# Attention units two at a time: transposes, evictions and values reordered in the first stage of a fused attention and MLP kernel

## The chip, the cores and the metric

The kernel runs on one core of a Trainium2 chip. Its time is the device time of one execution, in microseconds (us). The engines are TensorE (PE in the profile; its weight loads are listed apart as PEld), VectorE (DVE), ScalarE (ACT), GpSimd (POOL) and SyncE (SP, which issues the DMAs). Each engine takes its instructions in the order of its own queue and waits on semaphores for the others. [...]

## What is computed

An attention block with a bias that depends on position, then an MLP with a squared ReLU. Cut to what matters:

```python
B, H, S, D = 4, 8, 576, 64            # hidden size of the bias net 32
scores = q @ k.T / sqrt(D)
x = log1p(abs(i - j)) / log1p(max(i, 1))
bias = relu(x[..., None] @ w1 + b1) @ w2      # one value per head, i, j
attn = softmax(scores + bias)
x = (attn @ v) reordered to (B * S, H * D)
out = relu(x @ w_in) ** 2 @ w_out             # (2304, 512), d_ff 2048
```

## The kernel before

The attention is cut into 80 **units** (b, hp, ic): a batch, a pair of heads and a chunk of 128 query rows. The fifth chunk (`TAIL`) has only 64 rows and holds both heads in one tile. The first 40 units (`NA`) belong to batches 0 and 1 and run chunk by chunk: units 0 to 7 are tail chunks, units 8 to 15 chunk 0, and so on to unit 39. The other 40 units belong to batches 2 and 3 and run in a second stage, in which the preparation of the MLP's weights is mixed in. The MLP follows.

One unit goes through these steps. `score_products` (L404) puts the scores of two heads into four PSUM banks (tile `sp`, one buffer) with eight instructions of 64 rows each, both row halves of TensorE at once. `softmax` (L426) then does two things per head: a VectorE instruction (L431) adds the bias, keeps the result in `t` (two buffers) and finds the maximum, and a ScalarE instruction (L436) takes the exponential into `p` and sums it up. Two units later `transposes` (L494) turns `p` with nine 128 by 128 transposes on TensorE into three banks (`pp` twice with four each, `pa` with one), and ScalarE copies each to `pt` (L802). One unit later `values` (L511) multiplies `pt` by `v` into a bank `px` with twenty instructions of 64 columns each, both column halves of TensorE at once, and VectorE copies the result out (L530, ScalarE for units 0 to 7). After the last chunk of a head pair the sums are inverted, split into three bf16 parts by GpSimd, turned into rows by TensorE (L461), spread by TensorE (L483) and multiplied in by VectorE (L489).

The **bias** is made beside this, for 72 blocks (ic, jb) of 128 rows by 32 columns, `todo` in the code. `bias_mask` (L359) compares distances with thresholds on VectorE and leaves a 0/1 mask (three buffers). `bias_sum` (L374) multiplies the mask by weights on TensorE (16 instructions into a bank `bb`), ScalarE evicts one half with a scale (L386), VectorE multiplies the other half by position factors `xc` (L387), and GpSimd adds both into the bias table (L395). `bias_upto` (L560) makes the mask of the next block ahead of the sum of each block. Units of one chunk need all 18 blocks of that chunk.

In the stage of the first 40 units, the loop at L788, the order on each engine is left to the scheduler of the framework, which moves instructions past each other where data allow it. PSUM has eight banks: four hold `sp`, four are one rotating set for `bb`, `pp`, `pa`, `px` and the rest. The second stage (L966) stands under `tc.manual_schedule()`: there each engine takes the instructions in the order of the program, and the four banks have fixed names a, b, c and d. Jobs of the second stage are placed by `fill` (L833), which holds a budget of time per engine and step.

Of the kernel before, what the change touches and what calls it, by code (L numbers as in the profile page):

```python
# [77 lines left out]
def attention_then_relu2_mlp(ctx: ExitStack, tc: tile.TileContext, q, k, v, cols, w_in, w_out, psi, xmat, dist, out):  # L78
# [13 lines left out]
    def bank(name, tag=None):  # L92
        if tag is None:
            return bank_p["p"].tile([128, 512], F32, name=name, tag="aux", bufs=4)
        return bank_p["p"].tile([128, 512], F32, name=name, tag=tag, bufs=1)
# [275 lines left out]
        DVE.tensor_tensor(out=out, in0=win, in1=th, op=ALU.is_ge)  # L371
        mask_t[ic, jb] = m

    def bias_sum(ic, jb):  # L374
        m = mask_t.pop((ic, jb))
        bb = bank("bb")
        t = prep.tile([128, H, 32], F32, name="bt1", tag="bt1", bufs=BB)
        s = prep.tile([128, H, 32], F32, name="bt2", tag="bt2", bufs=BB)
        for r in range(8):
            for n in range(2):  # L380
                PE.matmul(bb[:, 64 * (7 - r):64 * (8 - r)], lhsT=m[:, r], rhs=wmov[:, n], start=(n == 0), stop=(n == 1))  # L381
        xv = xc_t[ic][:, 32 * jb:32 * jb + 32].rearrange("p (g j) -> p g j", j=4).unsqueeze(1)
# [4 lines left out]
        DVE.tensor_tensor(out=tv, in0=bv[:, 0], in1=xv.to_broadcast([128, H, 8, 4]), op=ALU.mult)  # L387
        if ic == TAIL:
# [6 lines left out]
        POOL.tensor_tensor(out=dst, in0=tw, in1=sw, op=ALU.add)  # L395

    def tail_bias(x, e, lo, hi, copy):
        src = tail_sum[64 * x:64 * x + 64, HP * e:HP * e + HP, lo:hi]
# [24 lines left out]
                tc.keep_in_program_order(mm)  # L423
        return negm, sps

    def softmax(u, n, negm, sp):  # L426
        b, hp, ic = units[u]
        p, sums = p_t[u], sum_t[b, hp]
        bias = bias_t[:, 9 * hp + 2 * ic + n]
        t = att.tile([128, S], F32, name="t", tag="t", bufs=TB)  # L430
        DVE.tensor_tensor_reduce(  # L431
            out=t.rearrange("p (x n) -> p x n", x=2), in0=sp[:, :, :HALF],
            in1=bias.rearrange("p (x n) -> p x n", x=2), scale=-0.125, scalar=3.0e38,
            op0=ALU.add, op1=ALU.min, accum_out=negm[:, n:n + 1],
        )
        ACT.activation(out=p[:, S * n:S * n + S], in_=t, func=AF.Exp, bias=negm[:, n:n + 1], scale=-1.0, accum_out=sums[:, 2 * ic + n:2 * ic + n + 1])  # L436
        if ic == TAIL:
            POOL.tensor_copy(out=p[:, S:S + 64], in_=p[:, S - 64:S])

    begun = {}  # L440

# [49 lines left out]
    def scale_x(b, hp, rows_t):  # L491
        times_rows(b, hp, *spread_rows(rows_t))

    def transposes(u, tags=(None, None, None)):  # L494
        n = 2 if units[u][2] < TAIL else 1
        p = p_t.pop(u)
        pt = att.tile([128, 9, 128], F32, name="pt", tag="pt", bufs=2)
        copies = []
        for h in range(n):
            pp = bank("pp", tags[h])  # L500
            for c in range(4):
                k0 = h * (S + 64) + 128 * c
                PE.transpose(pp[:, 128 * c:128 * c + 128], p[:, k0:k0 + 128], ident)  # L503
            copies.append((pt[:, 4 * h:4 * h + 4], pp.rearrange("p (c m) -> p c m", c=4)))
        pa = bank("pa", tags[2])
        PE.transpose(pa[:, :128], p[:, S - 64:S + 64], ident)  # L506
        copies.append((pt[:, 8], pa[:, :128]))
        pt_t[u] = pt
        return copies

    def values(u, tag=None):  # L511
        b, hp, ic = units[u]
        pt, vt = pt_t.pop(u), v_t[b, hp]
        w = 64 if ic == TAIL else 128
        px = bank("px", tag)
        for c in range(5):
            for h in range(2):
                if c == 4:
                    src = pt[:, 8, 64 * h:64 * h + 64] if ic == TAIL else pt[:, 8, :w]
                else:  # L520
                    src = pt[:, c, 64 * h:64 * h + 64] if ic == TAIL else pt[:, 4 * h + c, :w]
                PE.matmul(px[64 * h:64 * h + 64, :w], lhsT=vt[:, c, h], rhs=src, start=(c == 0), stop=(c == 4))  # L522
        end = S if ic == TAIL else 128 * ic + 128
        return xT[b][:, hp, end - w:end], px[:, :w]

    def keep_values(u, dst, src):
        if u < XC:
# [30 lines left out]
    done = 0  # L558

    def bias_upto(n):  # L560
        nonlocal done
        while done < min(n, len(todo)):
            if done + 1 < len(todo):
                bias_mask(*todo[done + 1])
            bias_sum(*todo[done])
            done += 1

    with tc.manual_schedule():
        late, main = theta_steps(512, S), theta_steps(0, 512)[:2] + theta_steps(0, 128)[2:]
# [215 lines left out]
        return ic == (chunks[-1] if u < NA else NIC - 1)  # L785

    rest = theta_steps(128, 512)[2:]
    for s in range(NA):  # L788
        loads(s)
        scores(s)  # L790
        if s and rest:
            tc.keep_in_program_order(rest.pop(0)())
        if s < AB * HP * TAIL:
            n, r = divmod(s, AB * HP)
            if r == 7 and n + 2 < NIC:
                tc.keep_in_program_order(scale_xc(chunks[n + 2]))
            bias_upto(NJB * n + BO[r])
            if r == 1 and n + 2 < NIC:
                load_xc(chunks[n + 2])
        if s >= TL:  # L800
            for dst, src in transposes(s - TL):
                ACT.copy(dst, src)  # L802
        u = s - TL - 1
        if u >= 0:
            keep_values(u, *values(u))
            b, hp, ic = units[u]
            if ends(u):
                waiting.append((b, hp, normalise(b, hp)))
            if waiting and waiting[0][:2] != (b, hp):
                scale_x(*waiting.pop(0))  # L810

    prep_stack.close()
    half_stack.close()
    aux_stack.close()
    bank_stack = ExitStack()
    bank_p["p"] = bank_stack.enter_context(tc.tile_pool(name="bank", bufs=1, space=PSUM, reuse_waits="tile"))
    pre = ctx.enter_context(tc.tile_pool(name="pre", bufs=1, side="left", reuse_waits="tile"))
# [4 lines left out]
    jobs, norms = [], []  # L822
    room = {}

    def lag(a, b):
# [23 lines left out]

    def norm_job(u):  # L850
        b, hp, ic = units[u]
        st = {"s": sum_t.pop((b, hp))}
        job(
            u + 1,
            ("DVE", 0.4, lambda: norm_inverse(st["s"])),
            ("POOL", 1.3, lambda: st.update(parts=norm_parts(st["s"])), u + TL + (u < NA)),
            ("ROW", 0.24, lambda: st.update(rows=norm_copy(norm_rows(st["parts"], "c"))), u + TL + 2 + (u < NA)),
            ("PE", 0, lambda: st.update(r=spread_rows(st["rows"], ("a", "b"))), u + TL + 2 + (u < NA)),
            ("LAST", 0.9, lambda: times_rows(b, hp, *st["r"])),
        )  # L860
        jobs.insert(len(norms), jobs.pop())
        norms.append(jobs[len(norms)])
# [27 lines left out]
    def scaled(ps_col):  # L890
        wscale.extend(power_of(ps_col))
        for n in range(AB):
            job(now[0] + 1, ("DVE", 0.16, lambda n=n: power_job(now[0] + 1, overall(xcols[n]), lambda c: x_scaled(n, c))))

    xcols = [column(HP) for _ in range(AB)]

    def x_job(at, n):
        job(at, *(("DVE", 0.67, lambda c=c: x_largest(n, xcols[n], (c,))) for c in range(HP)))

    def x_scaled(n, ps_col):  # L900
        scale_of(n, ps_col)
# [64 lines left out]
    with tc.manual_schedule():  # L966
        job(NA + 1, *(("DVE", 0.68, lambda k=k: scan(k)) for k in range(NF)))
        x_job(NA + 4, 0)
        x_job(NA + 7, 1)
        for u in range(NA - TL - 1, NA):  # L970
            norm_job(u)
        for s in range(NA, NU + TL + 2):
            now[0] = s
            full = s < NU and units[s][2] < TAIL
# [6 lines left out]
            if s < NU:  # L981
                negm, sps = score_products(s, False)
            fill(s, 3)
            copies = transposes(s - TL, ("a", "b", "c")) if s - TL < NU else []
            for n in range(2):
                for c in copies[n:n + 1 if n == 0 else None]:
                    ACT.copy(*c)  # L987
                if n:
                    px = values(s - TL - 1, "d") if s - TL - 1 < NU else None
# [8 lines left out]
            fill(s, 1)  # L998
            fill(s, 2)
            if px:  # L1000
                keep_values(s - TL - 1, *px)
    assert not jobs
    kq_stack.close()
    att_stack.close()
# [266 lines left out]
```

## Time and profile before

| | us |
|---|---|
| median of three runs | 731.0 (730.5 to 731.05) |
| the profiled execution | 731.07 |
| its span, first to last instruction | 729.0 |
| TensorE busy in the span | 701.5 |
| VectorE busy | 554.2 |
| ScalarE busy | 474.9 |
| GpSimd busy | 183.0 |
| granted clock of TensorE, mean | 0.992 |

How to read it: a row of the timeline begins with its start in us from the span's beginning, then its length in us, the engine, the line of the kernel, the operation, output and inputs, the shape, and how many instructions are merged. In square brackets stands how long the engine had been idle just before, and what released it. "Issue" is time in which the engine waited for nothing that the profile shows. Matmuls are pipelined, so each of them lasts longer than the distance to the next start. Distances between starts are what they cost in a row.

### The profile page before, as it was taken

Reading aid. Unit: us, or ns where it says so; the run is one execution under the profiler, and the core shown is the slowest. Engines: PE = TensorE matmul, PEld = TensorE weight load, DVE = VectorE, ACT = ScalarE, POOL = GpSimd, SP = SyncE. Lnnn points to the kernel's source line nnn. Section 1 sums busy time; section 2 is a strip of 40 time slices with the busy share of each in tenths; the row PEclk is TensorE's granted clock in tenths of the full one; section 3 lists DMA queues with packets and bytes.
Section 4 is the critical chain, followed back from the end, with each engine's and each line's share of the span. In section 5 each row is a group of like instructions: output and inputs, shape, how many; then the busy total and the mean of one; then the engine's idle time right before and its main releaser. Section 6 shows DMA issues by size and latency. Waiting matters only on the chain.

```text
span 729.0 us, 17376 instructions
## 1 busy us (share of the span) xinstructions
PE 701.5 (96%) x6966; PEld 565.1 (78%) x6966; DVE 554.2 (76%) x1181; ACT 474.9 (65%) x954; POOL 183.0 (25%) x297
## 2 busy tenths in 40 slices
PE   7799999999999999999999999999999999999992
PEld 6577777777777776777878888888888888888881
DVE  8998888865588789898898969868568775567661
ACT  5678777777677788888667657676465664454220
POOL 6563333331110146343421403212021112000000
PEclk9999999999999999999999999999999999999996
DMA  6630000004467421400623324050057313533100
GB/s 186 204 115 3 18 2 3 2 2 120 164 235 251 105 86 52 131 31 30 215 90 160 144 115 160 1 218 1 1 187 284 117 49 113 205 116 116 58 2 29
DMA packets 31620, 75.13 MB, mean 103 GB/s; under 512 B 5556, under 2 KB 13876, under 8 KB 30516
## 3 DMA queue, kind: packets, MB, share of 16 engines
q1 hardware_dynamic: 31540, 74.03, 29.7%
q8 instruction: 55, 0.90, 0.5%
q14 instruction: 25, 0.20, 0.1%
HBM read 55.66 MB, written 18.35 MB: 102 GB/s over the span
## 4 chain that ended last, share of the span: by engine, by line
PE 85%; DVE 8%; ACT 3%; issue 2%; DMA 0%; ACTq 0%; DVEq 0%
PE y L1147 26%; PE ha L1052 12%; PE px L522 11%; PE sp L421 11%; PE hb L1052 9%; PE pp L503 9%; PE bb L381 4%; DVE mask L371 2%; PE pa L506 2%; ACT p L436 1%; DVE t L431 1%; DVE bt L387 1%; ACT pt L987 1%; PE ra L483 1%; DVE wa L198 0%
## 5 line engine op out<-in xcount | busy, mean ns | idle before, releaser
L1052 PEld LDWEIGHTS <-area 128*128 128x128 f16 x1680 | 147.7, 98 | 24.8 <-issue 8.8
L1147 PE MATMUL y<-w,gh 128*128 128x512 f32 x576 | 149.2, 398 | 1.1 <-ACT gh L1091 1.1
L431 DVE CUSTOM_DVE_ANT_0 t<-sp,area 128x576 f32<-128x576 f32 x144 | 103.7, 754 | 27.7 <-PE sp L421 24.2
L1147 PEld LDWEIGHTS y<-w,gh 128*128 128x128 f32 x576 | 105.1, 188 | 23.3 <-ACT gh L1091 2.1
L436 ACT ACTIVATE p<-t,negm 128x576 f32<-128x576 f32 x144 | 111.9, 779 | 11.0 <-DVE negm L431 10.7
L421 PE MATMUL sp<-k,q 64*128 64x288 f32 (+1 forms) x640 | 98.6, 425 | 0.9 <-DVE negm L431 0.4
L522 PE MATMUL px<-pt,v 128*64 128x128 f32 (+1 forms) x1600 | 96.8, 267 | 1.5 <-DVE bt L387 0.7
L522 PEld LDWEIGHTS px<-pt,v 128*64 128x64 f32 x1600 | 79.2, 137 | 16.5 <-issue 6.9
L1052 PE MATMUL ha<-area 128*128 128x256 f16 (+1 forms) x816 | 85.4, 260 | 0.0
L503 PE MATMUL pp<-ident,p 128*128 128x128 f32 x576 | 82.4, 280 | 1.3 <-DVE bt L387 1.0
L1147 PE MATMUL y<-w,gl 128*128 128x512 f32 x288 | 79.0, 390 | 0.0
L503 PEld LDWEIGHTS pp<-ident,p 128*128 128x128 f32 x576 | 61.5, 141 | 19.7 <-issue 7.2
L395 POOL TENSOR_TENSOR area<-bt,bt 128x256 f32<-128x256 f32 x72 | 53.6, 767 | 78.5 <-DVE bt L387 78.5
L421 PEld LDWEIGHTS sp<-k,q 64*128 64x128 f32 (+1 forms) x640 | 52.6, 175 | 20.4 <-issue 6.8
L1052 PE MATMUL hb<-area 128*128 128x256 f16 (+1 forms) x612 | 64.9, 260 | 0.0
L1147 PEld LDWEIGHTS y<-w,gl 128*128 128x128 f32 x288 | 54.1, 188 | 12.2 <-DVE gl L1092 0.2
L987 ACT COPY pt<-pp 128x512 f32<-128x512 f32 x76 | 44.0, 579 | 27.7 <-PE pp L503 27.4
L371 DVE TENSOR_TENSOR mask<-sdist,theta 128x1024 f16<-128x1024 f16 x81 | 55.9, 727 | 5.6 <-PE bb L381 5.3
L381 PEld LDWEIGHTS <-mask 128*128 128x128 f16 x1296 | 42.3, 100 | 12.2 <-DVE mask L371 6.7
L381 PE MATMUL bb<-wmov,mask 128*128 128x64 f16 x1296 | 47.5, 196 | 4.3 <-DVE mask L371 4.1
L802 ACT COPY pt<-pp 128x512 f32<-128x512 f32 x68 | 37.7, 587 | 14.5 <-PE pp L503 14.5
L1092 DVE TENSOR_TENSOR gl<-area,gh 128x512 fp32r<-128x512 f32 (+1 forms) x40 | 25.3, 668 | 26.0 <-ACT gh L1091 24.2
(163 smaller groups left out, 987.8 us busy)
## 6 DMA issues: line engine op xcount, KB each, us to landing
raw<-in_w_in SPq DMA_DIRECT2D x32, 512.0 KB, 4.3
r<-in_w_out SPq DMA_DIRECT2D x16, 512.0 KB, 5.1
xs<-area SPq DMA_DIRECT2D x4, 1792.0 KB, 13.3
py<-o SPq DMA_DIRECT2D x12, 512.0 KB, 3.5
o<-py SPq DMA_DIRECT2D x12, 512.0 KB, 4.3
v<-in_v SPq DMA_DIRECT2D x16, 320.0 KB, 4.1
q<-in_q SPq DMA_DIRECT2D x32, 128.0 KB, 2.8
out<-o SPq DMA_DIRECT2D x8, 512.0 KB, 2.9
```

Source lines behind the costliest of these rows:

```text
L371: DVE.tensor_tensor(out=out, in0=win, in1=th, op=ALU.is_ge)
L381: PE.matmul(bb[:, 64 * (7 - r):64 * (8 - r)], lhsT=m[:, r], rhs=wmov[:, n], start=(n == 0), stop=(n == 1))
L395: POOL.tensor_tensor(out=dst, in0=tw, in1=sw, op=ALU.add)
L421: mm = PE.matmul(out_t[to, x, :HALF], lhsT=qt[rows, cols], rhs=kt[rows, k0:k0 + HALF], start=True, stop=True)
L431: DVE.tensor_tensor_reduce(out=t.rearrange("p (x n) -> p x n", x=2), in0=sp[:, :, :HALF], in1=bias.rearrange("p (x n) -> p x n", x=2), sca ...
L436: ACT.activation(out=p[:, S * n:S * n + S], in_=t, func=AF.Exp, bias=negm[:, n:n + 1], scale=-1.0, accum_out=sums[:, 2 * ic + n:2 * ic + n ...
L503: PE.transpose(pp[:, 128 * c:128 * c + 128], p[:, k0:k0 + 128], ident)
L522: PE.matmul(px[64 * h:64 * h + 64, :w], lhsT=vt[:, c, h], rhs=src, start=(c == 0), stop=(c == 4))
L802: ACT.copy(dst, src)
L987: ACT.copy(*c)
L1052: PE.matmul(h[:, s, :w], lhsT=a, rhs=x, start=(k == 0), stop=(k == 5))
L1147: PE.matmul(y_t[n][k], lhsT=(gl if m == 2 else gh)[:, slot, o:o + 128], rhs=wl if m == 1 else wh, start=((n, P) in firsts and f == 0 and m ...
```

## The change

Units 0 to 7 keep the old loop. For units 8 to 39 there is a new loop under a manual schedule, with the PSUM banks named: d for `pa` and `px`, and a, b, c in turn (`abc`) for `pp`, `bb` and the row products. Each even step does the scores of its unit, the transposes of the two units before it (both last transposes into one bank d, in front of the copies of both) and four or five bias blocks between them, with their evictions. The two exponentials of the even unit come behind the evictions of the first blocks. Each odd step does the scores and the exponentials of its unit, and then the values of two units into bank d. The masks run two or three blocks ahead of the sums. Row normalisation goes two units at a time as well. The stage after it takes over the last four normalisations.

```diff
+    def mask_upto(n):
+        nonlocal made
+        while made < min(n, len(todo)):
+            bias_mask(*todo[made])
+            made += 1
...
-    for s in range(NA):
+    for s in range(AB * HP):
...
+    def block(limit, ahead=3):
+        nonlocal done
+        if done < limit:
+            at, m, bb = bias_products(*todo[done])
+            bias_add(*at, *bias_parts(*at, bb))
+            done += 1
+        mask_upto(done + ahead)
+
+    with tc.manual_schedule():
+        for s in range(AB * HP, NA):
+            loads(s)
+            n, r = divmod(s, AB * HP)
+            if r == 1 and n + 2 < NIC:
+                load_xc(chunks[n + 2])
+            negm, sps = score_products(s, False)
+            ts = [softmax_max(s, h, negm, sp) for h, sp in enumerate(sps)]
+            if s == AB * HP:
+                for piece in values((s - 3,), "d"):
+                    keep_values(*piece)
+            if s % 2:
+                for h, t in enumerate(ts):
+                    softmax_exp(s, h, negm, t)
+                if r == 5 and n + 2 < NIC:
+                    scale_xc(chunks[n + 2])
+                pieces = values((s - 3, s - 2), "d")
+                mask_upto(done + 2)
+                for piece in pieces:
+                    keep_values(*piece)
+                mask_upto(done + 3)
+                for b, hp, rows_t in waiting:
+                    times_rows(b, hp, *spread_rows(rows_t, (abc(), abc())))
...
+                        norm_inverse(z)
+                        ended.append((b, hp, norm_parts(z)))
+            else:
+                blocks = min(20 + 13 * (s - 6) // 6, len(todo))
+                copies = transposes((s - 2, s - 1), iter(abc, None))
+                for c in copies if s < AB * HP + 2 else (next(copies), next(copies)):
+                    ACT.copy(*c)
+                block(blocks)
+                for c in copies:
+                    ACT.copy(*c)
+                block(blocks)
+                block(blocks, 2)
+                softmax_exp(s, 0, negm, ts[0])
+                while done < blocks:
+                    block(blocks, 2)
+                softmax_exp(s, 1, negm, ts[1])
+                for b, hp, parts in ended:
+                    waiting.append((b, hp, norm_copy(norm_rows(parts, abc()))))
+                ended.clear()
```

`softmax_max` and `softmax_exp` are the two halves of the former `softmax`. `bias_products`, `bias_parts` and `bias_add` are the parts of the former `bias_sum`. `transposes` takes a list of units now and yields each copy once its transposes are issued: three groups of four, then the two last transposes of both units, then the fourth group. `values` takes a list of units and puts unit m into columns 128 m of one bank.

## Rows read from the trace of the kernel before

**Rows 1.** The page: busy time by engine, and the chain that ended last.
```profile
PE 701.5 (96%) x6966; PEld 565.1 (78%) x6966; DVE 554.2 (76%) x1181; ACT 474.9 (65%) x954; POOL 183.0 (25%) x297
...
PE 85%; DVE 8%; ACT 3%; issue 2%; DMA 0%; ACTq 0%; DVEq 0%
```

**Rows 2.** Table by stretch: bounds, length, busy us (instructions) per engine, clock, DMA.
```profile
52.20:58.90 6.70, 6.68 (x116) 5.17 (x115) 5.48 (x15) 5.57 (x16) 2.41 (x4) 1.00 0.06 19
58.90:161.93 103.03, 102.88 (x1599) 81.98 (x1599) 84.79 (x207) 82.59 (x212) 36.34 (x51) 1.00 0.02 5
161.93:199.00 37.07, 36.49 (x409) 27.61 (x408) 20.21 (x63) 26.76 (x70) 4.94 (x25) 1.00 0.43 139
```

**Rows 3.** Timeline of TensorE, 94 to 105 us: one step and its neighbours.
```profile
96.90 0.14 PEld L506 LDWEIGHTS pa<-ident,p 128*128 128x128 f32 x1 [0.39 <-issue]
96.90 0.33 PE L506 MATMUL pa<-ident,p 128*128 128x128 f32 x1
...
97.16 1.31 PE L522 MATMUL px<-pt,v 128*64 128x128 f32 x20
...
98.40 1.57 PE L381 MATMUL bb<-wmov,mask 128*128 128x64 f16 x48
...
99.81 0.63 PE L503 MATMUL pp<-ident,p 128*128 128x128 f32 x4
...
100.38 1.24 PE L421 MATMUL sp<-k,q 64*128 64x288 f32 x8
...
101.55 0.66 PE L503 MATMUL pp<-ident,p 128*128 128x128 f32 x4
...
102.04 0.27 PE L506 MATMUL pa<-ident,p 128*128 128x128 f32 x1
...
102.25 1.31 PE L522 MATMUL px<-pt,v 128*64 128x128 f32 x20
```

**Rows 4.** The same timeline, ScalarE: evictions, copies, exponentials.
```profile
99.35 1.20 ACT L386 ACTIVATE bt<-bb,small 128x256 f32<-128x256 f32 x3
...
102.24 0.58 ACT L802 COPY pt<-pp 128x512 f32<-128x512 f32 x1 [1.17 <-PE pp L503]
...
102.72 0.27 ACT L802 COPY pt<-pa 128x128 f32<-128x128 f32 x1
102.88 0.79 ACT L436 ACTIVATE p<-t,negm 128x576 f32<-128x576 f32 x1
...
103.65 0.77 ACT L436 ACTIVATE p<-t,negm 128x576 f32<-128x576 f32 x1
```

**Rows 5.** The same timeline, VectorE: masks, multiplications, maxima.
```profile
99.08 1.90 DVE L371 TENSOR_TENSOR mask<-sdist,theta 128x1024 f16<-128x1024 f16 x3 [0.27 <-PE bb L381]
...
100.89 1.08 DVE L387 TENSOR_TENSOR bt<-bb,xc 128x256 f32<-128x256 f32 x3
...
101.89 0.75 DVE L431 CUSTOM_DVE_ANT_0 t<-sp,area 128x576 f32<-128x576 f32 x1
...
102.56 0.76 DVE L431 CUSTOM_DVE_ANT_0 t<-sp,area 128x576 f32<-128x576 f32 x1
```

**Rows 6.** Timeline, 155 to 159 us: an eviction and the multiplication behind it.
```profile
156.66 1.20 ACT L386 ACTIVATE bt<-bb,small 128x256 f32<-128x256 f32 x3
...
157.14 1.17 DVE L387 TENSOR_TENSOR bt<-bb,xc 128x256 f32<-128x256 f32 x3 [1.02 <-ACT bt L386]
```

**Rows 7.** Timeline of TensorE, 53 to 55 us: values of a tail unit.
```profile
53.40 0.80 PE L522 MATMUL px<-pt,v 128*64 128x64 f32 x20
54.14 0.64 PE L381 MATMUL bb<-wmov,mask 128*128 128x64 f16 x16
```

**Rows 8.** Timeline of TensorE, 192 to 193 us: row products, then a transpose.
```profile
192.22 0.23 PE L461 MATMUL rp<-ident_b,parts 128*27 128x128 bf16 x1
...
192.84 0.33 PE L503 MATMUL pp<-ident,p 128*128 128x128 f32 x1
```

**Rows 9.** DMA issues on the page: KB each, us to landing.
```profile
v<-in_v SPq DMA_DIRECT2D x16, 320.0 KB, 4.1
```

More of the change, by code (lines that the diff above doesn't have):

```diff
@@ L372, in bias_mask, with bias_products @@
         mask_t[ic, jb] = m
-    def bias_sum(ic, jb):
+    def bias_products(ic, jb):
         m = mask_t.pop((ic, jb))
-        bb = bank("bb")
-        t = prep.tile([128, H, 32], F32, name="bt1", tag="bt1", bufs=BB)
-        s = prep.tile([128, H, 32], F32, name="bt2", tag="bt2", bufs=BB)
+        bb = bank("bb", abc() if bank_p.get("pairs") else None)
         for r in range(8):
@@ L492, in scale_x @@
         times_rows(b, hp, *spread_rows(rows_t))
[L494 to L514, printed above, removed]
-        px = bank("px", tag)
[L516 to L524, printed above, removed]
+    def transposes(us, tags=None):
+        next_tag = iter(tags) if tags else None
+        groups = []
+        pa = None
+        for m, u in enumerate(us):
+            p_of = p_t.pop(u)
+            pt = att.tile([128, 9, 128], F32, name="pt", tag="pt", bufs=2)
+            pt_t[u] = pt
+            for h in range(2 if units[u][2] < TAIL else 1):
+                groups.append((p_of, pt, h))
+            groups.append((p_of, pt, None, m))
+        if len(us) > 1:
+            heads = [g for g in groups if g[2] is not None]
+            groups = heads[:3] + [g for g in groups if g[2] is None] + heads[3:]
+        last = []
+        for p, pt, h, *m in groups:
+            if h is None:
+                if pa is None:
+                    pa = bank("pa", "d" if tags and len(us) > 1 else next(next_tag) if tags else None)
+                at = slice(128 * m[0], 128 * m[0] + 128)
+                PE.transpose(pa[:, at], p[:, S - 64:S + 64], ident)
+                last.append((pt[:, 8], pa[:, at]))
+                if len(last) == len(us):
+                    yield from last
+            else:
+                pp = bank("pp", next(next_tag) if tags else None)
+                for c in range(4):
+                    k0 = h * (S + 64) + 128 * c
+                    PE.transpose(pp[:, 128 * c:128 * c + 128], p[:, k0:k0 + 128], ident)
+                yield pt[:, 4 * h:4 * h + 4], pp.rearrange("p (c m) -> p c m", c=4)
@@ new lines, in values @@
+    def values(us, tag=None):
+        px = bank("px", tag)
+        pieces = []
+        for m, u in enumerate(us):
+            b, hp, ic = units[u]
+            pt, vt = pt_t.pop(u), v_t[b, hp]
+            w = 64 if ic == TAIL else 128
+            for c in range(5):
+                for h in range(2):
+                    if c == 4:
+                        src = pt[:, 8, 64 * h:64 * h + 64] if ic == TAIL else pt[:, 8, :w]
+                    else:
+                        src = pt[:, c, 64 * h:64 * h + 64] if ic == TAIL else pt[:, 4 * h + c, :w]
+                    PE.matmul(px[64 * h:64 * h + 64, 128 * m:128 * m + w], lhsT=vt[:, c, h], rhs=src, start=(c == 0), stop=(c == 4))
+            end = S if ic == TAIL else 128 * ic + 128
+            last = pieces[-1] if pieces else None
+            if last and last[1] == (b, hp) and last[3] == end - w:
+                last[3], last[4] = end, 128 * m + w
+            else:
+                pieces.append([u, (b, hp), end - w, end, 128 * m + w, 128 * m])
+        return [(u, xT[b][:, hp, x0:x1], px[:, c0:c1]) for u, (b, hp), x0, x1, c1, c0 in pieces]
@@ L800, in attention_then_relu2_mlp @@
         if s >= TL:
-            for dst, src in transposes(s - TL):
+            for dst, src in transposes((s - TL,)):
                 ACT.copy(dst, src)
[L803 to L813, printed above, removed]
+        if s > TL:
+            for piece in values((s - TL - 1,)):
+                keep_values(*piece)
     aux_stack.close()
@@ L969, in attention_then_relu2_mlp @@
         x_job(NA + 7, 1)
-        for u in range(NA - TL - 1, NA):
+        for u in range(NA - TL - 2, NA):
             norm_job(u)
+            if ended:
+                jobs[len(norms) - 1][1][:2] = []
+                parts_of[units[u][:2]] = ended.pop(0)[2]
         for s in range(NA, NU + TL + 2):
@@ L983, in attention_then_relu2_mlp @@
             fill(s, 3)
-            copies = transposes(s - TL, ("a", "b", "c")) if s - TL < NU else []
+            copies = list(transposes((s - TL,), ("a", "b", "c"))) if s - TL < NU else []
             for n in range(2):
```

58 lines of the change are left out of this document (45 added, 13 removed).

## Prediction

> **What bounds the kernel now.** I read the page first: TensorE is busy 701.5 of 729.0 us, and the chain of work that ended last is 85% TensorE [rows 1]. Then the table by stretches. The change lies between the score products of unit 8 (52.20 us) and those of unit 41 (199.00 us), the first that both kernels reach with the same units behind them. There TensorE stands still 0.02 of 6.70 us, 0.15 of 103.03 us and 0.58 of 37.07 us, while VectorE and ScalarE are busy some 80% in the long middle stretch [rows 2]. So TensorE's instruction stream sets the pace, and only what shortens that stream, or makes it wait, moves the end.
>
> Third, one step in order of time [rows 3]. From start to start: the scores take 1.17 us until the next kind, the values (px) 1.24, 48 masked products (bb) 1.41, which is 0.029 each or 0.47 per block of 16. A transpose costs 0.11 behind another transpose ((0.66 - 0.33)/3, and a lone one that follows scores lasts 0.33). But one transpose between scores and values takes 0.26, against 0.11, and four transposes ahead of scores take 0.57 against some 0.47. The weight load is late (0.39 us idle ahead of the lone transpose) where the shape of the product changes: 64-row scores, 128-row transposes and masked products, 64-column values. A step with two blocks lasts 4.62 us (5.09 from px to px with three, less 0.47).
>
> **The change: changes of shape saved.** Before, two units go px, bb, pp, sp, pa, px, ...: eight changes. After, a pair is: scores of the even unit, all 18 transposes with the masked products among them, scores of the odd unit, values of two units: four changes. Its TensorE time without waits, with four blocks: 1.17 (scores) + 0.49 (four transposes behind scores, [rows 3]) + 0.44 + 0.47 (block 1) + 0.47 (four transposes behind a block) + 0.22 (two last transposes) + 0.44 + 1.41 (blocks 2 to 4) + 0.09 (change) + 1.17 + 2.34 (values: 1.24, and ten more column pairs at 0.11) = 8.71 us. Before it is 2 x 4.62 = 9.24, so 0.53 is saved; with five blocks 9.18 against 9.71. The formula for `blocks` gives four to the pairs at s = 8, 10, 14, 16, 20, 22, 26, 28 and five to s = 12, 18, 24, 30.
>
> **New waits, from a walk through one pair.** Zero is the start of the even scores. ScalarE's pitches: copy 0.48, small copy 0.16, exponential 0.77, eviction of a block 0.37 with an end at 0.46 [rows 4]. VectorE's: mask 0.60 (done at 0.69), multiplication 0.33, maximum 0.67 (done at 0.75) [rows 5]. A multiplication begins only when ScalarE's eviction of the same bank has ended: VectorE idled 1.02 us for it [rows 6]. Handing on costs about 0.04.
>
> [...]
>
> ScalarE: first copy at 1.86, second 2.34, eviction 1 at 2.84 (ends 3.30), third copy 3.24, small copies 3.72 and 3.88, last copy 4.03, eviction 2 at 4.51 (ends 4.97), eviction 3 at 4.95, exponential 5.31, eviction 4 at 6.08 (ends 6.54), second exponential 6.44 to 7.3.
> VectorE: two maxima until 2.7, multiplication 1 at 3.33, mask 3.66 to 4.35 (that of block 4), multiplication 2 at 5.00, multiplication 3 at 5.44, multiplication 4 at 6.57, a mask 6.90 to 7.50, then the two maxima of the odd unit at 7.50 and 8.17, done 8.93.
> TensorE: block 2 is free to go at 3.70 but its bank (three turn round) is read until 3.75: 0.10 lost. Odd scores 5.30, values 6.47, ready for the next even scores at 8.80, but these wait for the odd maxima: 8.98. What is queued behind is TensorE's whole stream. **Four blocks: 8.98 against 9.24, -0.26; seven pairs: -1.8.**
>
> With five blocks the mask of block 5 stands behind multiplication 2 in VectorE's queue: 5.33 to 6.02. TensorE is ready for block 5 at 5.21 and gets it at 6.07: 0.86 idle, with the odd scores behind it. The rest moves along: values until 10.13, maxima done 9.9, no second wait. **10.13 against 9.71, +0.42; four pairs: +1.7.** That the evictions go ahead of the exponentials helps here (an exponential in front would add 0.77), but the maxima of the odd unit need both exponentials' buffers and stand behind more of the queue.
>
> **First pair.** The loop before leaves a mask for only one block ahead. So at s = 8 block 2's mask comes behind multiplication 1, which comes behind one eviction and five copies on ScalarE: by the same walk block 2 starts 2.0 us late, and the maxima of unit 9 hold the scores of unit 10 by 0.9 more. I get 10.94 us from scores to scores. The work itself would take 7.9: the 6.70 of [rows 2], without one short values step (0.74, [rows 7]), with two more and a block. +3.0; if work left from the free-ordered loop (one values step) fills part of the hole, +2.3. I take **+2.6**.
>
> **Units 32 to 40.** No blocks: a pair takes 1.17 + 0.49 + 0.44 + 0.44 + 0.22 + 0.44 + 0.09 + 1.17 + 2.34 = 6.80. Each row normalisation puts 0.62 us on TensorE [rows 8] and there are four until unit 41, one fewer than before. In pairs they load VectorE at once: the multiplications by the spread rows and the inverses of two units stand behind the two copies, so the maxima of units 38 and 40 come some 0.8 us late, and the second row product waits about 1 us for GpSimd's parts in the pair at s = 38. Walked through, unit 32 to unit 41 takes 34.6, and 0.6 for the fifth normalisation comes later. Before: 37.07 [rows 2], less two values steps which the new order has done by unit 32 (2.5), 34.6. **+0.6.**
>
> At nothing I cost: the load of the next bias factors, issued at the same unit as before and scaled four units (18 us) later, against 4.1 us for the nearest load [rows 9]; its scaling, two units earlier, falls into ScalarE's idle time behind the odd exponentials (0.8 to 1.8 us per pair; without that cover 0.72 twice); and the second stage, whose conditions only change the place of small jobs (bounds -1 to +1).
>
> Sum: -1.8 + 1.7 + 2.6 + 0.6 = +3.1. The profiled execution took 731.07 us (span 729.0), 0.07 above the median: 734.1, said as **734.0**. A size of 0.1 us in each walk is 1.2 us on the sum.
>
> **Rivals.**
> *Faster: VectorE is not last.* If masks and multiplications arrive before TensorE asks (the mask of block 5 by 5.1 us, the odd maxima by 8.7), the savings stay. For it: VectorE and ScalarE have some 20% idle [rows 2]. Against it: both are in order, and the mask stands behind a wait that [rows 6] shows. With no wait left but the first pair's start: 11 x 0.53 = 5.8, less about 0.5 at the ends: 725.5; with multiplications beside evictions only: 729. Taken as 727. Chance 0.26.
> *No change.* The waits as walked, but the first pair's hole is filled and the last pairs hide their normalisations: 731.1 - 0.1 + 0.7 = 731.7. It needs leftover work of the old loop in the right place. Chance 0.24.
> *Slower still.* The maxima also decide the five-block pairs (0.2 us of room only), or each hand-over costs 0.1 rather than 0.04: 12 x 0.25 more, 737. Chance 0.05.
> *The change doesn't do what it says:* the lost time belongs to the instructions, not to the change of shape. Then the waits remain without the gain, 734 + 7.5 = 741. Transposes behind masked products, no change of shape, show nothing of it [rows 3]. Chance 0.02.
> *The clock falls.* [...] Chance 0.01.
>
> **How the numbers follow.** My forecast (732.5 to 736) has 0.42. About 0.2% (1.5 us) is what a measurement of this kernel can tell from none. Faster 0.26, within 0.24, slower 0.50. The range of 8 in 10 runs from 726.5, inside the faster rival, to 736.5. Both signs hold much, so the forecast's own range stands here too: 732.5 to 736.
>
> **What would show it.** Right: in the profile after, TensorE waits for masks (L371's line) about 0.9 us in four pairs and 2 us at unit 8, and for the maxima about 0.2 us at even scores; scores-to-scores distances of 9.0 and 10.1 us per pair, 6.8 without blocks. The weight loads' idle rows before values and scores halve in number. Wrong: pairs of 8.7 us with no wait on masks (then the saving stands whole), multiplications that start before the eviction of their bank ends, or a distance that is long with TensorE busy.

## The result, and the profile after

The changed kernel takes 739.34 us (median of four runs, 738.61 to 740.21) beside 730.84 (730.50 to 731.05) for the kernel before: a ratio of 1.0116, 95% interval 1.0103 to 1.0129. It is slower, as forecast, but by 8.5 us where 3.0 were said, and outside the stated range of 732.5 to 736. The profiled execution took 739.66 us with a span of 737.9, 8.9 more than before.

The page of the kernel after, busy time by engine and the chain that ended last:

```profile
PE 698.4 (95%) x6966; PEld 568.5 (77%) x6966; DVE 555.2 (75%) x1181; ACT 474.9 (64%) x954; POOL 197.5 (27%) x297
...
PE 72%; DVE 13%; ACT 8%; issue 3%; DMA 2%; POOL 0%; ACTq 0%; DVEq 0%; SPq 0%
```

Beside [rows 1]: TensorE has the same 6966 instructions and 3.1 us less to do, and its share of the chain fell from 85% to 72%; VectorE and ScalarE took ten of the thirteen points that it lost. One engine is busier for the same work: GpSimd, 197.5 against 183.0 us.

The table by stretches, from unit 8 to 10, to unit 32, to unit 41 (bounds, length, busy us of PE, PEld, DVE, ACT, POOL, TensorE's granted clock as a share of full speed, DMA share, GB/s):

```profile
52.26:64.77 12.51, 10.15 (x172) 8.04 (x171) 8.78 (x20) 7.53 (x22) 5.43 (x6) 0.86 0.03 10
64.77:172.86 108.09, 100.60 (x1587) 85.32 (x1583) 84.45 (x202) 82.45 (x208) 48.14 (x48) 1.00 0.02 5
172.86:206.56 33.70, 31.86 (x360) 25.22 (x358) 20.08 (x70) 23.09 (x63) 3.97 (x21) 1.00 0.46 144
```

Unit 41 starts at 206.56, 7.56 us later than in [rows 2]: nearly the whole loss lies in the stage of the new loop. TensorE, idle 0.15 us of the long stretch before, is idle 7.49 us of it now. What it waited for there (waits, 64.77 to 172.86; us in total, times, longest):

```profile
PE sp L431 <- DVE negm L440: 4.4, 10, 0.5
...
PE bb L379 <- DVE mask L371: 3.0, 4, 0.8
```

Ten even scores waited for the maxima of the odd unit before them, and four bias blocks for their masks: the two waits that the prediction walked to. The first had been put at 0.18 us, in the four-block pairs alone; it is 0.52 there, and 0.26 behind three of the five-block pairs.

From even scores to even scores, the pairs of units last, in the middle stretch, 9.41 to 9.47 us with four blocks (forecast 8.98) and 10.6 with five (10.13). The one at s = 30 lasts 10.27; it has no masks left to make at its end, and its next scores wait for nothing. The first pair takes 12.51, and the pairs without blocks begin with two of 6.79. One four-block pair in order of time (start, length, idle before and its releaser in brackets):

```profile
84.77 1.24 PE L431 MATMUL sp<-k,q 64*128 64x288 f32 x8 [0.27 <-DVE negm L440]
...
89.83 0.42 DVE L390 TENSOR_TENSOR bt<-bb,xc 128x256 f32<-128x256 f32 x1 [0.69 <-ACT bt L389]
...
90.17 0.68 DVE L371 TENSOR_TENSOR mask<-sdist,theta 128x1024 f16<-128x1024 f16 x1
90.33 2.94 POOL L401 TENSOR_TENSOR area<-bt,bt 128x256 f32<-128x256 f32 x3 [0.60 <-DVE bt L390]
90.77 0.42 DVE L390 TENSOR_TENSOR bt<-bb,xc 128x256 f32<-128x256 f32 x1
...
91.41 0.42 DVE L390 TENSOR_TENSOR bt<-bb,xc 128x256 f32<-128x256 f32 x1 [0.23 <-ACT bt L389]
91.76 0.92 DVE L371 TENSOR_TENSOR mask<-sdist,theta 128x1024 f16<-128x1024 f16 x1
...
92.60 0.74 DVE L440 CUSTOM_DVE_ANT_0 t<-sp,area 128x576 f32<-128x576 f32 x1
...
94.18 1.24 PE L431 MATMUL sp<-k,q 64*128 64x288 f32 x8 [0.52 <-DVE negm L440]
```

Between the multiplications of blocks 2 and 3 (89.83 and 90.77) VectorE makes a mask that the walk had left out. The mask behind the last multiplication takes 0.92 us, with GpSimd's adds beside it. The odd maxima begin at 92.60, 7.83 us into the pair where the walk had 7.50, and the next scores come at 94.18, 0.52 us late.

### The profile page after: what moved, and what is told of

Its sections match the earlier page's. It is cut to its first block, busy times and chain, and to the rows that moved or that the text cites. A ratio compares the mean times of both kernels' runs of the same rounds, so it can differ in the third digit from the quotient of the medians.

```text
span 737.9 us, 17326 instructions
## 1 busy us (share of the span) xinstructions
PE 698.4 (95%) x6966; PEld 568.5 (77%) x6966; DVE 555.2 (75%) x1181; ACT 474.9 (64%) x954; POOL 197.5 (27%) x297
## 4 chain that ended last, share of the span: by engine, by line
PE 72%; DVE 13%; ACT 8%; issue 3%; DMA 2%; POOL 0%; ACTq 0%; DVEq 0%; SPq 0%
PE y L1259 26%; PE ha L1164 12%; PE hb L1164 9%; PE sp L431 9%; PE px L555 7%; PE pp L539 6%; DVE mask L371 3%; DVE t L440 3%; ACT bt L389 3%; DVE bt L390 2%; DMA raw<-in_w_in 2%; ACT pt L910 2%; ACT pt L907 1%; PE bb L379 1%; ACT p L450 1%
## 5 line engine op out<-in xcount | busy, mean ns | idle before, releaser
L555 PE MATMUL px<-pt,v 128*64 128x128 f32 (+1 forms) x1600 | 93.5, 267 | 2.0 <-DVE xT L568 1.2
L401 POOL TENSOR_TENSOR area<-bt,bt 128x256 f32<-128x256 f32 x72 | 68.7, 975 | 75.3 <-DVE bt L390 75.2
L1098 ACT COPY pt<-pp 128x512 f32<-128x512 f32 x76 | 44.0, 579 | 28.7 <-PE pp L539 28.5
L371 DVE TENSOR_TENSOR mask<-sdist,theta 128x1024 f16<-128x1024 f16 x81 | 60.6, 759 | 0.2
L379 PEld LDWEIGHTS <-mask 128*128 128x128 f16 x1296 | 44.2, 100 | 16.9 <-DVE mask L371 13.2
L390 DVE TENSOR_TENSOR bt<-bb,xc 128x256 f32<-128x256 f32 x81 | 33.4, 418 | 21.4 <-ACT bt L389 21.4
L389 ACT ACTIVATE bt<-bb,small 128x256 f32<-128x256 f32 x81 | 38.0, 474 | 13.8 <-PE bb L379 9.7
```

Of the source, the lines that this page charges most:

```text
L555: PE.matmul(px[64 * h:64 * h + 64, 128 * m:128 * m + w], lhsT=vt[:, c, h], rhs=src, start=(c == 0), stop=(c == 4))
```

## The experiments

Two theories stood. **V:** VectorE's order is at fault: masks stand in its queue ahead of the odd maxima and behind multiplications that wait for evictions. **G:** GpSimd's adds now run beside the masks and each holds up the other. The third question was whether the saving from fewer changes of shape is real. Except where a line says otherwise, an edit is made to the kernel after, and the ratios are to the kernel before. Pair lengths are from even scores to even scores.

### Masks behind the maxima

```diff
-                    block(blocks, 2)
+                    block(blocks, 0)
```

The second call of the two, in the `while` loop: the masks behind the last blocks move behind the odd maxima, to the odd step's own `mask_upto`.

> The fourth and fifth block of a pair make no mask; the odd step makes two or three behind its two copies. Theory V (VectorE's order: the mask behind the last multiplication stands before the odd maxima, and those hold the next scores): the four-block pair falls from 9.41 to about 8.8 us, the five-block pair from 10.60 to about 10.3, in all 5 to 6 us less, 734 us. Theory G (it is GpSimd's adds that stretch the masks, 0.25 us each): about 9.15 and 10.4, 737 us. Theory S (ScalarE's order alone sets the pair): no change, 739 us.

Measured: 732.72 us (732.47 to 733.86), ratio 1.0027 (1.0016 to 1.0038). Four-block pairs 8.82 to 8.88, five-block pairs 10.27 and 10.26. The table's first two stretches:

```profile
52.60:64.18 11.58, 8.66 (x172) 7.11 (x171) 8.09 (x19) 7.51 (x22) 5.05 (x6) 1.00 0.03 9
64.18:167.10 102.92, 99.85 (x1582) 84.51 (x1582) 82.42 (x203) 82.38 (x208) 42.33 (x48) 1.00 0.02 5
```

No wait for the maxima is left in the long stretch; the four for masks remain at the 3.0 us of the kernel after. This is V. It also shows the saving of the pair: 8.82, where the walk had TensorE ready at 8.80 and two units of two blocks took 9.24 before. But G is undone in part too: no mask takes more than 0.69 us here. And 0.93 of the gain, 11.58 instead of 12.51, lies in the first pair, where the granted clock stayed at 1.00 (below).

### Masks ready at unit 8

```diff
+    mask_upto(done + 3)
     with tc.manual_schedule():
```

> Two more masks are made ahead of unit 8. If the first pair is long because block 2 waits for its mask, and its second scores are slow (2.2 us, granted clock 0.86 in this stretch) because TensorE stood still before them: the first pair falls from 12.5 to about 9.6 us with the clock at 1.00, 736.5 us. If the slow clock has another cause: about 10.6 us with the clock still below 1. If block 2 waits for ScalarE: no change, 739 us.

Measured: 736.93 us (736.52 to 737.34), ratio 1.0082 (1.0067 to 1.0097). First pair 10.59 rather than 12.51, at a granted clock of 1.00; the others as after (9.41 and 10.60). So the two masks were worth 1.9 us of the 2.9 that had been expected. Block 4 still waits 0.93 us for its mask, and the next scores 1.29 for the odd maxima, behind a long mask:

```profile
60.10 1.24 DVE L371 TENSOR_TENSOR mask<-sdist,theta 128x1024 f16<-128x1024 f16 x1
...
62.84 0.52 PE L431 MATMUL sp<-k,q 64*128 64x288 f32 x2 [1.29 <-DVE negm L440]
```

### Exponentials in front of the evictions

```diff
+                softmax_exp(s, 0, negm, ts[0])
+                softmax_exp(s, 1, negm, ts[1])
                 block(blocks)
                 block(blocks, 2)
-                softmax_exp(s, 0, negm, ts[0])
                 while done < blocks:
                     block(blocks, 2)
-                softmax_exp(s, 1, negm, ts[1])
```

> The third part of the change undone: both exponentials of the even unit stand ahead of the evictions of blocks 2 to 5. By the walk through a pair, evictions 2 to 5 and the multiplications behind them come 1.5 us later, the last multiplication 0.7: four-block pairs 9.8 to 10.0 us, five-block pairs 11.4, together some 6 us more, 745 us. If evictions and exponentials only fill ScalarE's idle time: no change, 739 us.

Measured: 763.6 us (two runs, 762.06 and 765.14), ratio 1.0447 (1.042 to 1.0474). Pairs of 10.90 at the least and of 12.4 to 13.4 in five places, well above the 9.8 to 11.4 expected. Two pairs of four blocks in the table by stretches, and from TensorE's timeline the scores behind the first of them:

```profile
64.37:75.27 10.90, 8.89 (x138) 7.56 (x139) 7.27 (x18) 7.21 (x22) 4.04 (x4) 1.00 0.01 3
98.23:110.74 12.51, 10.48 (x138) 8.75 (x139) 7.67 (x20) 7.22 (x20) 4.03 (x4) 0.86 0.00 1
```

```profile
75.28 0.52 PE L431 MATMUL sp<-k,q 64*128 64x288 f32 x2 [2.02 <-DVE negm L440]
```

The scores wait 2.0 us for the maxima, and in the second of these pairs, longer still, the granted clock is 0.86 on average, a fall that I had not put in. The place of the evictions, ahead of the exponentials, is thus worth some 24 us in this order of the loop, the stretches at a lower clock included, and it is not what made the kernel slower.

### No add on GpSimd

```diff
-        POOL.tensor_tensor(out=dst, in0=tw, in1=sw, op=ALU.add)
+        if ic and bank_p.get("pairs"):
+            POOL.memset(dst, 0.0)
+        else:
+            POOL.tensor_tensor(out=dst, in0=tw, in1=sw, op=ALU.add)
```

The bias of chunks 1 to 3 is left out.

> The sum of both bias halves is left out for chunks 1 to 3 from unit 8 on: GpSimd writes zeros instead, so the bias of these chunks is missing. Theory G (GpSimd's adds stretch VectorE's masks): masks all at 0.68 us, four-block pairs 9.41 to 9.15, five-block pairs 10.60 to 10.35, the first pair shorter by 0.5, together 3.4 us less, 736.3 us. Theory V: the masks shorten, the pairs by at most 0.1 us, 738.5 us.

Measured: 738.95 us (738.88 and 739.02), ratio 1.011 (1.009 to 1.013). The time says nothing, since without these adds the scheduler ordered the loop before otherwise, and unit 8 began at 48.04 with a first pair of 19.66. The pairs behind it do: 9.16 to 9.22 with four blocks and 10.27 with five, against 9.41 to 9.47 and 10.6. All 46 masks of that stretch take 681 to 689 ns. So the adds beside the masks are worth 0.25 us of a four-block pair and 0.33 of one with five; without them the pair is 0.2 longer than forecast still.

### Masks in front of the multiplications

```diff
-    def block(limit, ahead=3):
+    def block(limit, ahead=3, early=False):
...
             at, m, bb = bias_products(*todo[done])
+            if early:
+                mask_upto(done + 1 + ahead)
...
+    mask_upto(done + 3)
...
-                block(blocks)
+                block(blocks, 3, True)
                 block(blocks, 2)
...
-                    block(blocks, 2)
+                    block(blocks, 0)
```

The two edits of the first two experiments, and the new mask of block 2 in front of the multiplication of that block, not behind it.

> Three edits of the masks' place alone: two more ahead of unit 8, the second block's new mask in front of its multiplication (as soon as block 2's product has freed a mask buffer), and none in the fourth and fifth block. If VectorE's order is all that turned the gain into a loss: four-block pairs 8.8 us (9.24 before the change), five-block pairs 9.3 (9.71 before), the first pair about 9.3, 727 us, so faster than the kernel before the change by some 4 us. If the pairing itself costs as much elsewhere (bank d, three turning banks, the second stage): 731 us or more although the waits on masks and maxima are gone.

Measured: 729.77 us (729.35 to 731.04, eleven runs) beside 730.84, ratio 0.9987 (0.9978 to 0.9996): with the kernel of four blocks in each pair (below) the only order here that beats the kernel before, and by one microsecond. The stretches:

```profile
52.36:62.10 9.74, 8.36 (x172) 7.00 (x171) 7.52 (x19) 7.43 (x22) 4.87 (x7) 1.00 0.04 14
62.10:164.03 101.93, 99.83 (x1582) 84.80 (x1582) 86.13 (x203) 82.41 (x208) 38.15 (x49) 1.00 0.02 5
164.03:197.71 33.68, 31.86 (x360) 25.23 (x358) 20.09 (x70) 23.07 (x63) 3.94 (x21) 1.00 0.47 145
```

Four-block pairs 8.82 and 8.87 as expected, five-block pairs 10.01 and a first pair of 9.74, where 9.3 had been expected of both; unit 41 at 197.71, 1.3 us ahead of [rows 2]. A five-block pair is still 0.3 longer than before: its fifth mask waits less, and now the bank of a block is late (the wait of bb for VectorE's multiplication, 2.0 us in four pairs).

### Values of the two units apart

To the kernel of the experiment before, one unit's values in each step:

```diff
-            if s == AB * HP:
+            if s % 2 == 0:
                 for piece in values((s - 3,), "d"):
                     keep_values(*piece)
...
-                pieces = values((s - 3, s - 2), "d")
+                pieces = values((s - 3,), "d")
```

> As e5_masks_in_place, but the values of the two units are taken apart again: one behind the odd scores, one behind the next even scores, which is five changes of product shape in a pair and not four. If a change of shape costs what the rows of before say: every pair 0.15 to 0.2 us longer than in e5_masks_in_place, some 3 us in all. If the lost time belongs to the instructions: no difference.

Measured: 742.53 us, ratio 1.0158 (1.0142 to 1.0173). Four-block pairs 9.29 once and then 9.86 to 9.95, five-block pairs 10.63: up to 1.1 more, where 0.15 to 0.2 had been expected. Its waits (62 to 175 us):

```profile
PE sp L431 <- DVE negm L440: 8.0, 12, 1.0
```

Most of it is a wait that the edit brought with it. With twenty products rather than forty behind the odd scores, TensorE comes to the even scores before the odd maxima are made. The values of two units are what covers those maxima.

What the change of shape itself costs can be read from start to start, first here and then in the first experiment, in a pair without waits:

```profile
92.10 1.24 PE L431 MATMUL sp<-k,q 64*128 64x288 f32 x8 [0.76 <-DVE negm L440]
93.27 1.31 PE L555 MATMUL px<-pt,v 128*64 128x128 f32 x20
94.51 1.09 PE L539 MATMUL pp<-ident,p 128*128 128x128 f32 x8
```

```profile
88.58 1.24 PE L431 MATMUL sp<-k,q 64*128 64x288 f32 x8
89.75 2.40 PE L555 MATMUL px<-pt,v 128*64 128x128 f32 x40
92.08 1.24 PE L431 MATMUL sp<-k,q 64*128 64x288 f32 x8
```

Twenty products apart take 1.24 us, as before the change, so twice twenty take 2.48; forty together take 2.33. One group of values fewer saves 0.15, as expected.

### Last transposes apart

To the same kernel: each last transpose's copy comes directly behind it, and the second one waits for the bank.

```diff
-                last.append((pt[:, 8], pa[:, at]))
-                if len(last) == len(us):
-                    yield from last
+                yield pt[:, 8], pa[:, at]
```

> As e5_masks_in_place, but each of the two last transposes stands ahead of its own copy alone. They share a bank, so the second waits until ScalarE has copied the first: TensorE stands still 0.9 us behind the first, pairs 9.6 to 9.7 us instead of 8.8, 16 pairs, about 13 us more. If the transposes of the second unit could fill that time: no change.

Measured: 742.56 us (742.12 and 743.0), ratio 1.016 (1.0141 to 1.0178). Four-block pairs 9.64 to 9.67 rather than 8.82, as expected (five-block pairs 10.48 rather than 10.01). The new wait (64 to 170 us):

```profile
PE pa L531 <- ACT pt L911: 8.1, 11, 0.7
```

Both last transposes in front of their copies save 0.8 us per four-block pair: with the two apart, TensorE waits for the copy of the first before the second goes into the same bank, the 8.1 us in 11 waits above.

### Multiplication in front of the eviction

```diff
-        ACT.activation(out=sv, in_=bv[:, 1], func=AF.Identity, scale=bscale)
         DVE.tensor_tensor(out=tv, in0=bv[:, 0], in1=xv.to_broadcast([128, H, 8, 4]), op=ALU.mult)
+        ACT.activation(out=sv, in_=bv[:, 1], func=AF.Identity, scale=bscale)
```

In the new loop alone.

> As the changed kernel, but from unit 8 on VectorE's multiplication of a block stands ahead of ScalarE's eviction of the same bank; masks as in the changed kernel. If VectorE was late because its multiplications wait for ScalarE: the masks behind them come earlier, four-block pairs 9.41 to 8.9 us, five-block pairs 10.60 to 9.7 to 10.0, 731 to 733 us. If only the order of masks and maxima on VectorE matters: 9.3 and 10.5, 738 us. The wait turns round, and ScalarE waits for the multiplications instead.

Measured: 733.93 us (733.81 to 734.23), ratio 1.0042 (1.0027 to 1.0057). Expected were 731 to 733. Five-block pairs take 9.65 to 9.71, about as expected, four-block ones 9.18 to 9.25 (one 9.6) where 8.9 had been expected. The wait has changed sides (64 to 170 us):

```profile
ACT bt L391 <- DVE bt L390: 8.8, 23, 0.5
...
DVE t L444 <- ACT p L454: 5.1, 15, 0.4
```

Now evictions wait for the multiplications, ScalarE's exponentials come later behind them, and the maxima wait for the buffers that the exponentials free. In either order the engine that reads the bank second waits: in the kernel after it is VectorE, 16.4 us in 34 waits (64.77 to 172.86). In none of the 81 blocks of the kernel before or of the kernel after do the eviction and the multiplication overlap.

### Four blocks in each pair

To the kernel with the masks in place: the units before 8 make 24 blocks rather than 20, and each pair four.

```diff
-BO, B1 = (3, 5, 8, 10, 13, 15, 18, 20), (12, 3, 8)
+BO, B1 = (3, 5, 8, 10, 13, 16, 20, 24), (12, 3, 8)
...
-                blocks = min(20 + 13 * (s - 6) // 6, len(todo))
+                blocks = min(24 + 2 * (s - 6), len(todo))
```

(The factors of the next chunk are scaled two units earlier in the loop before.)

> As e5_masks_in_place, but the loop of units 0 to 7 makes 24 blocks and not 20, with the factors of the second chunk scaled two units earlier, so that every pair has four blocks. If the five-block pairs lose time only because a fifth block needs a mask in mid-pair: 12 pairs of 8.8 us, four times 10.01 - 8.82 = 1.19 us less in the pairs, and four blocks (0.47 us each) more in the first loop, 727 us. If the first loop is held by VectorE, which makes four masks and multiplications more there (1 us each): 729 to 730 us, no gain over e5_masks_in_place.

Measured: 729.79 us (729.39 to 730.94, eleven runs), ratio 0.9987 (0.9978 to 0.9996): the same as with five-block pairs. All later pairs with blocks take 8.82 to 8.88 but one of 9.15; unit 8 begins at 53.32 and the first pair takes 13.13. Four blocks moved forward cost there what they save later. This is the second of the two forecasts by its time; that VectorE is what holds the first loop is not shown.

### Masks in place, no add

The kernel with the masks in place, with the edit on GpSimd's add (the bias of chunks 1 to 3 left out).

> As e5_masks_in_place with the sum of both bias halves left out for chunks 1 to 3 from unit 8 on (GpSimd writes zeros, so the bias of these chunks is missing). The mask in mid-pair, 1.02 us there, comes back to 0.68; if GpSimd's adds make up what the five-block pairs still lose: 10.01 to about 9.6 us, four-block pairs as they are (8.8). If TensorE waits there for a bank and not for the mask: 9.9 to 10.0.

Measured: 732.13 us, one run, with the order of the loop before changed again (first pair 17.87). Four-block pairs 8.82 and 8.87 as with the adds, five-block pairs 9.68 rather than 10.01. So 0.33 of a five-block pair are the adds beside the masks even here. In this trace TensorE waits in these pairs for a bank alone (0.7 us in four, for VectorE's multiplication), and for no mask: block 5 starts 0.82 behind block 4 rather than 0.47. Without this wait the pair is 9.33, against the walk's 9.18 and 0.10 for a bank.

## Why the prediction was right or wrong

**Right: what bounds, and where it would wait.** TensorE's stream set the pace; the saving from fewer changes of shape is real (8.82 without waits against 9.24; forecast 8.71, and 8.80 with the bank's wait; the sixth experiment prices one change at 0.15, and in the long stretch the weight loads stood idle ahead of values in 22 places before, 0.12 to 0.38 us each, and 11 after, 0.38 each, ahead of scores in 22 and 11); the eviction and the multiplication take turns at a bank (16.4 us of VectorE's waits in the long stretch after; the eighth experiment turned the order round and found 8.8 us of waits on the other engine); masks of the fifth block and of unit 8 were late; a pair without blocks takes 6.79 (6.80). The rival "doesn't do what it says" falls by the first experiment, "the clock falls" by the granted 1.00 of the two later stretches, with 18 transposes per pair, in runs of 8 and 10 where there are blocks and of 18 where there are none. The 729 of the faster rival, with multiplications beside evictions, is an estimate whose case no run shows: before and after, the two take turns in all 81 blocks. "Slower still", by maxima that also decide the five-block pairs and by dearer hand-overs, had 0.05 and came nearest in mechanism.

**Wrong, the term of the four-block pair: -0.26 was said, +0.19 measured.** Seven of them: +1.3, not -1.8. The step that failed is the walk of VectorE's queue, which gave the even scores a wait of 0.18. They waited about 0.6 (the distance from the first experiment's 8.82 to 9.41), 0.4 more, from three things:

- The walk put multiplication 3 directly behind multiplication 2. By the code a mask stands between, and the trace has it at 90.17. ScalarE's pace hid most of that: the last multiplication came 6.64 into the pair, not 6.57 (0.07).
- The mask behind the last multiplication took 0.92, not 0.69, and the odd maxima began 0.84 behind its start, not 0.60 (0.24). The walk took its durations from [rows 5], in which masks and adds hardly met: from unit 8 on, two masks of 50 ran beside an add before (one of them for 0.03 us) and 39 of 51 after. The fourth experiment prices the adds at 0.25 of the 0.6.
- From the end of the maximum's read-out to the scores took 0.14, not 0.05 (0.09).

**Wrong, the five-block pair: +0.42 was said, +0.81 measured.** Four of them: +3.2, not +1.7. The hole of the fifth block was about as forecast: the block starts 1.38 behind block 4 and not 0.47, 0.91 late against 0.86 (the idle rows have 0.75, since a block's products last 0.63 us and the next start follows 0.47 behind theirs). The step "no second wait" failed: with the maxima as late as above, the next scores waited 0.33 more. The pair at s = 30, in which no mask stands ahead of the odd maxima, lacks this wait, and so do all in the first experiment.

**Too small, the first pair: +2.6 was said, +3.9 measured.** A values step left over from the old loop did run inside it, but ahead of the hole, so it filled nothing: 12.51 against 7.9 + 0.74 of work. The walk's hole ahead of block 2 is there: it starts 2.03 late from start to start (1.87 idle), and 2.0 were said. The 0.9 that the maxima of unit 9 were to cost is not. In its place stand two things that the walk did not have: block 3 waits 0.49 us for its mask, which took 1.22 us beside an add and not 0.68 (the second of the three below), and the clock fell behind these holes (the timeline of the kernel after, then the table of four stretches with its clock in the third last column):

```profile
57.69 2.42 DVE L371 TENSOR_TENSOR mask<-sdist,theta 128x1024 f16<-128x1024 f16 x3
57.85 1.10 POOL L401 TENSOR_TENSOR area<-bt,bt 128x256 f32<-128x256 f32 x1 [2.94 <-DVE bt L390]
...
58.43 0.64 PE L379 MATMUL bb<-wmov,mask 128*128 128x64 f16 x16 [1.87 <-DVE mask L371]
59.56 1.34 PE L379 MATMUL bb<-wmov,mask 128*128 128x64 f16 x32 [0.49 <-DVE mask L371]
...
60.83 2.29 PE L431 MATMUL sp<-k,q 64*128 64x288 f32 x8
```

```profile
60.00:61.00 1.00, 1.00 (x25) 0.83 (x22) 1.00 (x4) 0.70 (x2) 0.48 (x1) 0.77 0.00 0
61.00:62.00 1.00, 1.00 (x6) 0.72 (x8) 0.44 (x3) 1.00 (x4) 1.00 (x2) 0.50 0.00 0
62.00:63.00 1.00, 1.00 (x6) 0.30 (x2) 0.95 (x2) 0.65 (x2) 0.89 (x2) 0.50 0.00 0
63.00:64.00 1.00, 1.00 (x20) 0.95 (x20) 0.83 (x3) 0.03 (x1) 0.53 (x1) 0.52 0.00 0
```

The scores of unit 9 take 2.29 us at a granted clock of 0.50 rather than 1.24. The second experiment, without these two holes, has them at 1.24. In the first experiment the same two holes stand, the clock does not fall, the maxima then cost 0.56, and the pair takes 11.58: the clock is some 0.9 of the 1.3 that were missed.

**Units 32 to 41: +0.6 was said, -0.9 measured** (33.70 against the 34.6 of the kernel before). The walk had the maxima of units 38 and 40 some 0.8 late and a row product waiting about 1 us. No scores wait in this stretch; the row product waits 0.17, and what costs is VectorE's multiplying in of the spread rows, which TensorE waits for once for 0.59 and once for 0.97 us. The normalisation that is left for later costs about 1.0 between units 41 and 42, where 0.6 had been put. The ledger to unit 41: +1.3 + 3.2 + 3.9 - 0.9 = +7.5, measured 7.56.

**The second stage, "at nothing" within -1 to +1: +1.2** from unit 41 to 79 in the profiled execution, the 1.0 of that normalisation among it. A load took part as well. The raw weights wait for space that the keys of the first stage hold until its last scores: their second issue follows the last scores of unit 39 by 0.04 us, before (187.90), after (200.26) and in the fifth experiment (191.40). The first five issues, and the scan that reads one of these loads, in the kernel after:

```profile
188.49 13.52 SPq L684 DMA_DIRECT2D raw<-in_w_in  x5
...
235.32 0.69 DVE L202 TENSOR_REDUCE small<-raw 128x1 f32<-128x512 f32 x1 [1.59 <-DMA raw<-in_w_in]
```

Before, the five issues begin at 182.92 and take 6.74 us, and no scan waits. The scan's wait is 0.49 in the first experiment's trace and 1.90 in the fifth's, so it moves with details that I did not settle. The profiled execution of the fifth (1.3 us above its kernel's median) took 140.87 us from unit 41 to 79 against 139.38 before, and gave the 1.3 us won at unit 41 back.

## What to carry to other kernels

When work is regrouped so that TensorE changes shape less often, walk each other engine's queue with every instruction that the code issues, and look at what stands ahead of the result that the next group needs: here one line moved behind the maxima gave back 6.6 of 8.5 us, 0.9 of it by the clock in the first pair. Durations taken from a trace had the neighbours of that trace (a mask of 0.68 us took up to 1.22 here beside an add, an add of 0.73 up to 1.19 beside a mask); if the new order puts two engines beside each other that were apart, take a range for both, and walk which of the two begins second. And count the start of a new order as a term of its own, since prepared work that the old loop did not leave has to be paid for: the first pair was 3.9 us longer here, some 0.9 of it by the clock.

## What the runs showed of the hardware that was not expected

**GpSimd and VectorE side by side.** GpSimd's adds in the long stretch, after and then before (minimum, median and maximum ns, first and last start):

```profile
L401 POOL TENSOR_TENSOR area<-bt,bt x48: 722/1107/1188, 68.6 to 170.6; 128x256 f32<-128x256 f32 x48
```

```profile
L395 POOL TENSOR_TENSOR area<-bt,bt x51: 721/728/1104, 60.4 to 159.0; 128x256 f32<-128x256 f32 x51
```

The masks beside them, after and then before:

```profile
L371 DVE TENSOR_TENSOR mask<-sdist,theta x46: 672/681/930, 64.5 to 168.0; 128x1024 f16<-128x1024 f16 x46
```

```profile
L371 DVE TENSOR_TENSOR mask<-sdist,theta x48: 683/689/694, 58.7 to 152.4; 128x1024 f16<-128x1024 f16 x48
```

In the kernel with the masks in place they reach 1022. The adds are hit more often than the masks (35 of 48, against 13 masks that are clearly longer). Which of the two is hit goes by which begins second, in the kernel after from unit 8 on: all 38 adds that began inside a mask took 1.10 to 1.19 us and the other 16 took 0.72 to 0.74. The 24 masks that an add joined kept 0.67 to 0.68. Of the 15 masks that began inside an add, 14 took 0.88 to 1.22, longer by what was left of the add less some 0.13 us (0.38 left: 0.93; 0.67 left: 1.22), and one, with 0.05 left of the add, 0.68. Multiplications and maxima keep their 0.42 and 0.75 us beside adds in the pair shown above. Why the masks and not these are held up, no run shows.

**The clock after holes.** TensorE's granted clock fell to 0.50 for 3.4 us (60.55 to 63.96) behind holes of 1.87 and 0.49 us at unit 8 of the kernel after. In the first experiment holes of 1.86 and 0.49 us stand at the same place, and the clock stays at 1.00:

```profile
58.76 0.64 PE L379 MATMUL bb<-wmov,mask 128*128 128x64 f16 x16 [1.86 <-DVE mask L371]
59.89 1.24 PE L379 MATMUL bb<-wmov,mask 128*128 128x64 f16 x32 [0.49 <-DVE mask L371]
61.06 1.24 PE L431 MATMUL sp<-k,q 64*128 64x288 f32 x8
```

Within the third experiment, too, the pair behind the hole of 2.02 us at 75.28 keeps 1.00, while behind the pair that ends at 98.23, as long as the one that ends at 75.27 and with as much for TensorE to do (10.90 and 8.89 us), the clock falls (the 0.86 of the second pair above). What decides stays open. A hole of this size is therefore to be priced with and without the fall, here about 0.9 us between the two first pairs.
